# Local q and k of batches 4 to 7: loaded one token a row and transposed by DMA from SBUF instead of on TensorE

## The chip, the cores and the metric

The kernel runs on one core of one Trainium2 chip. The metric is the device time of one execution in microseconds (us); the time before is the median of three runs. Engines are called as the profile calls them: PE is TensorE (PEld its weight loads), DVE is VectorE, ACT is ScalarE, POOL is GpSimd, and SP is the engine whose queue issues most of the DMA transfers.

## What is computed

Attention with a fixed sparse mask is followed by two matrix products with a squared ReLU between them. There are 8 batches, 8 heads, 576 tokens and 64 numbers a head. Heads 0 to 3 are "local" (a token sees itself and the 31 before it), heads 4 to 7 are "strided" (it sees earlier tokens whose position is the same modulo 32).

```python
scores = scale * np.matmul(q, k.transpose(0, 1, 3, 2))
mask_local = (rel >= 0) & (rel < stride)                       # rel = query - key, stride = 32
mask_strided = (rel >= 0) & (pos[None, :] % stride == pos[:, None] % stride)
attn = softmax(np.where(masks, scores, -1e9))
x = np.matmul(attn, v).transpose(0, 2, 1, 3).reshape(4608, 512)
r = np.maximum(x @ w_in, 0.0)                                  # w_in 512 x 2048
out = (r * r) @ w_out                                          # w_out 2048 x 512
```

## The kernel before

**Units.** The attention is cut into 32 units, four a batch: unit u belongs to batch u // 4, and holds two heads. The first two of a batch are local (for batch 4, units 16 and 17), the last two strided. A unit goes through these steps, each a Python function that emits a few instructions:

- `step_T` (L188) turns q or k, which lie in SBUF with tokens on the partitions, so that the head's numbers lie on the partitions. For a local unit it is six PE transposes (L196) of 96 x 128 into PSUM, and one copy to SBUF: q by ACT (L209), k by DVE (L211) into one of the `kTl` tiles, which have 32 columns of zeros in front.
- `step_S` (L217) forms the scores: 12 (local) or 16 (strided) small matmuls (L240), exponentials on ACT (L245), masks on DVE (L251).
- `step_D` (L259), in two or three parts, multiplies with v (L276), and DVE divides by the sum (L287, L288).
- `step_E` (L291) turns the result and puts it into `xt`, the input of the matrix products: on PE for strided units (L305, copy L313), and for local units from batch 2 on by a DMA transpose from SBUF on the SP queue (L298, `xt<-x_l`).

**Loads.** `loads(b)` (L399) issues a batch's loads on SP: for each of the two local units q and k as float32 (L90, one transfer each for both heads; six consecutive tokens a partition, so that one row is 1536 bytes) and v (L137, two transfers, 256-byte rows, 96 tokens apart), then v of the strided units (L153). POOL casts them to bf16 (`cast_qk_local`, L98; L144, L145, L160). From batch 2 on the strided q and k are cast by a POOL-issued DMA into DRAM (L117), and `transpose_str` (L122) brings them back with two DMA transposes on SP (L125, `qT_s<-q_d` and `kT_s<-k_d`), the `strT` pool having two slots for each of q and k. In batches 0 and 1 strided q and k are loaded to SBUF (`load_qk_str`, L102, pool `qs_in`, two slots each) and go through `step_T`.

**Products.** The 4608 tokens are nine chunks of 512. `mm1` (L319) is one group of four 128x512 matmuls (L325), a ReLU on ACT (L328) and a square on DVE (L329); 16 such groups a chunk. `mm2` (L333) is one group of four matmuls (L340) of the second product; four of them fill one output tile of 128 rows, which ACT copies (L344) and SP stores (L346).

**Order.** The order of all engines is written by hand: what the program emits first comes first in each engine's queue, and each queue runs in that order, waiting for semaphores. There are 288 groups: chunk 0's `mm1` is groups 0 to 15, its `mm2` 16 to 31, chunk 1 has 32 to 63, chunk 2's `mm1` 64 to 79; from group 80 on `mm1` of chunk c and `mm2` of chunk c - 1 alternate, 32 groups for a chunk (80, 112, 144, 176, 208, 240). The attention steps of the batches 1 to 7 are one list (`stream_steps`, L375); `due` says how many of them stand before each group, spread evenly so that batch b's are all done where it is needed: batch 1 at group 32, batch 2 at 56, batch b from 3 on at the start of chunk b. In that list `step_T` of a local unit stands two units ahead of its scores, among the parts of `step_D`. `loads(b)` is called at group 8 for batch 2, and for b = 3 to 7 at groups 34, 58, 82, 114, 146; `transpose_str(b)` six groups later:

```python
        if n in load_at:
            loads(load_at[n])
            tr_at[n + 6] = load_at[n]
        if n in tr_at:
            transpose_str(tr_at[n])
        g()
```

SP's queue therefore holds, in program order, the loads, the y stores, the transposes of strided q and k and the `xt<-x_l` transposes.

Of the kernel before, what the change touches and what calls it, by code (L numbers as in the profile page):

```python
# [9 lines left out]
BF16 = mybir.dt.bfloat16  # L10
# [4 lines left out]
def kernel(  # L15
# [9 lines left out]
    nc = tc.nc  # L25
    B, H, S, D = q.shape
    d_model, d_ff = moe_w_in.shape
    T = B * S
# [3 lines left out]
    QL = 96  # L32
    NL = S // QL
    NJ = 8
    RH = STRIDE // NJ
    SP_ = RH * NA
# [3 lines left out]
    singles = ctx.enter_context(tc.tile_pool(name="singles", bufs=1))  # L40
    qk_st = ctx.enter_context(tc.tile_pool(name="qk_st", bufs=2))
    qk_in = ctx.enter_context(tc.tile_pool(name="qk_in", bufs=3))
    qs_in = ctx.enter_context(tc.tile_pool(name="qs_in", bufs=2))
    qkT = ctx.enter_context(tc.tile_pool(name="qkT", bufs=3))
    v_st = ctx.enter_context(tc.tile_pool(name="v_st", bufs=2))
    small = ctx.enter_context(tc.tile_pool(name="small", bufs=4))
# [4 lines left out]

    PS = bass.MemoryType.PSUM
    dram = ctx.enter_context(tc.tile_pool(name="dram", bufs=2, space=bass.MemoryType.DRAM))
    strT = ctx.enter_context(tc.tile_pool(name="strT", bufs=2))
    ps_h = ctx.enter_context(tc.tile_pool(name="ps_h", bufs=2, space=PS))
    ps_y = ctx.enter_context(tc.tile_pool(name="ps_y", bufs=1, space=PS))
# [4 lines left out]
    NV = 4  # L61
# [3 lines left out]
    vls = [singles.tile([128, 2, NL, VP], BF16, name=f"vl{i}") for i in range(NV)]  # L65
    vss = [singles.tile([SP_, NBS, VP], BF16, name=f"vs{i}") for i in range(NV)]
    vl_sts = [singles.tile([128, 2 * NL, D], FP32, name=f"vl_st{i}") for i in range(2)]
    kTl = [singles.tile([128, 32 + S], BF16, name=f"kTl{i}") for i in range(3)]
    es = [singles.tile([128, 1280], BF16, name=f"e{i}") for i in range(4)]
    xt = [singles.tile([128, T], BF16, name=f"xt{p}") for p in range(4)]  # L70
    w_in_b = singles.tile([128, 4, d_ff], BF16)
# [5 lines left out]
    units = [(b, p) for b in range(B) for p in range(H // 2)]  # L77
    st = {}

    def is_local(u):  # L80
        return units[u][1] < H // 4

    def load_qk_local(u, eng, gate=None):
        b, p = units[u]
        s = st.setdefault(u, {})
        for name, src in (("q", q), ("k", k)):
            t = qk_st.tile([QL, 2, 6 * D], FP32, name=f"{name}_st")
            if gate is not None and name == "q":
                nc.gpsimd.tensor_copy(t[0:1, 0, 0:1], gate)
            eng.dma_start(out=t, in_=src[b, 2 * p:2 * p + 2]  # L90
                          .rearrange("h (p j) d -> p h (j d)", j=6))
            s[name + "f"] = t
# [9 lines left out]
    def load_qk_str(u):  # L102
        b, p = units[u]
        s = st.setdefault(u, {})
        for name, src in (("q", q), ("k", k)):
            t = qs_in.tile([SP_, 2, NJ * D], BF16, name=f"{name}_s")
            nc.gpsimd.dma_start(out=t, in_=src[b, 2 * p:2 * p + 2]
                                .rearrange("h (p j) d -> p h (j d)", j=NJ))
            s[name] = t

    XB = 2
# [10 lines left out]
    def transpose_str(b):  # L122
        for name in "qk":
            o = strT.tile([128, NJ // 2, 4 * SP_], BF16, name=f"{name}T_s")
            nc.sync.dma_start_transpose(out=o, in_=big.pop((b, name)))  # L125
            for i in range(2):
                st.setdefault(4 * b + 2 + i, {})[name + "T"] = o[:, :, 2 * SP_ * i:2 * SP_ * (i + 1)]

    def v_slot(u):
        b, p = units[u]  # L130
        return (b * 2 + p % 2) % NV
# [52 lines left out]
    def tick():  # L184
        clock[0] += 1
        run_due(lambda x: x[0] <= clock[0])

    def step_T(u, name):  # L188
        s = st[u]
        local = is_local(u)  # L190
        n, w = (6, QL) if local else (NJ, SP_)
        src = s[name]
        src = src.rearrange("p j h d -> p (j h d)" if local else "p h c -> p (h c)")
        pt = ps_t.tile([128, S], BF16, name="pt")
        for j in range(n):
            nc.tensor.transpose(pt[:, w * j:w * (j + 1)], src[:, 128 * j:128 * (j + 1)],  # L196
                                ident[0:w, 0:w])
        if local and name == "k":
            full = kTl[u % 3]
            dst = full[:, 32:32 + S]  # L200
        else:
            full = dst = qkT.tile([128, S], BF16, name=f"{name}T")
        if local:
            o = dst.rearrange("c (p j) -> c p j", j=6)
            i = pt.rearrange("c (j p) -> c p j", j=6)
        else:
            o, i = dst, pt
        if name == "q":
            nc.scalar.copy(o, i)  # L209
        else:  # L210
            nc.vector.tensor_copy(o, i)  # L211
        s[name + "T"] = full
# [120 lines left out]
    def mm2(c, i, pool=None):  # L333
# [8 lines left out]
        if part == 3:  # L342
# [3 lines left out]
            nc.sync.dma_start(out=out[r0:r0 + 128, :], in_=y)  # L346

    T_ = lambda u, nm: (lambda: step_T(u, nm))
    S_ = lambda u: (lambda: step_S(u))
    D_ = lambda u, part: (lambda: step_D(u, part))  # L350
# [19 lines left out]
        return [(fn, 0 if i < n - 8 else 4) for i, fn in enumerate(order)]  # L370

    def has_T(u):
        return is_local(u) or units[u][0] < XB

    def stream_steps(lo, hi, base):  # L375
        order = [T_(lo, "q"), T_(lo, "k"), T_(lo + 1, "q"), S_(lo), T_(lo + 1, "k")]
        ends = {}
        for u in range(lo, hi + 1):
            if u < hi - 1:
                order.append(S_(u + 1))  # L380
            if u > lo:
                order.append(E_(u - 1))
                ends[u - 1] = base + len(order)
            if u < hi:
                order.append(D_(u, 0))
                if u + 2 < hi and has_T(u + 2):
                    order.append(T_(u + 2, "q"))
                order.append(D_(u, 1))
                if u + 2 < hi and has_T(u + 2):
                    order.append(T_(u + 2, "k"))  # L390
                if not is_local(u):
                    order.append(D_(u, 2))
        return order, ends
# [5 lines left out]
    def loads(b):  # L399
        u = 4 * b  # L400
        for i in range(2):
            load_qk_local(u + i, nc.sync, gate=gates.get(b) if i == 0 else None)
            load_v_local(u + i, nc.sync)
        load_v_str(u + 2, nc.sync)
        load_v_str(u + 3, nc.sync)
        w_out = load_w_out if b == 1 else (lambda i: None)
        if b >= XB:
            cast_str_dram(b)
        else:
            load_qk_str(u + 2)  # L410
        w_out(0)
        cast_qk_local(u, pool2)
        cast_v_local(u)
        if b < XB:
            load_qk_str(u + 3)
        w_out(1)
        cast_qk_local(u + 1, pool2)
        cast_v_local(u + 1)
        w_out(2)
        cast_v_str(u + 2)  # L420
        cast_v_str(u + 3)
        w_out(3)

    load_qk_local(0, nc.sync)
    load_qk_local(1, nc.sync)
    load_qk_str(2)
    make_identity(nc, ident)
    load_qk_str(3)
# [88 lines left out]
    load_at = {8: 2}  # L517
    tr_at = {}
# [10 lines left out]
    for n, g in enumerate(groups):  # L529
        while done < due[n]:  # L530
            steps[done]()
            done += 1
        if n in load_at:
            loads(load_at[n])
            tr_at[n + 6] = load_at[n]
        if n in tr_at:
            transpose_str(tr_at[n])
        g()
        tick()
    for _ in range(4):  # L540
# [31 lines left out]
```

## Time and profile before

| what | value |
|---|---|
| runs | 335.35, 336.91, 337.31 us; median 336.91 |
| profiled execution | 338.12 us, of which the span (first to last instruction) 336.3 |
| busy in the span | PE 305.6, DVE 175.3, ACT 167.6, POOL 88.7 us |
| L325 matmuls | 147.1 us recorded busy in 550 records |
| L340 matmuls | 100.7 us in 390 records and 41.6 us in 170 |
| L196, q of local units | 96 transposes, 7.4 us busy |
| L196, k of local units | 96 transposes, 7.5 us busy |
| L209 / L211 copies of local q / k | 0.64 us (ACT) / 0.75 us (DVE) each |
| DMA packets on the queue that SP uses | 54784, 33.63 MB |

The profiler records one execution; times within it are counted from the first instruction. In a timeline each line is a run of like instructions: start, length, engine, line of the code, operation, tile written and read, shape, count, and in brackets how long the engine had been idle and what ended that. A PE length is the time of one pass through a pipeline, so that lengths of neighbours overlap. "SPq" is SP's queue: the length there is that of the issue. A few matmul records are missing from the trace.

### The profile page before, as it was taken

To read this page: it belongs to the slowest core of one execution; us is meant where nothing else is said; L and a number is where in the kernel's file an instruction comes from. 1 tells how busy PE (TensorE), PEld (TensorE's weight loads), DVE (VectorE), ACT (ScalarE), POOL (GpSimd) and SP (SyncE) were. 2 spreads that over 40 slices of the span, in tenths; PEclk is the share of its full clock that TensorE was granted. 3 is DMA by queue.
4 is the path that set the end of the run, shared out by engine and by line. 5 is a ranking of instruction groups with operands and counts; after the bars stand their busy time and mean duration, and the time that the engine had idled before them with its cause. 6 is when DMAs were issued, how large, how long until landed. Compare 5 with 4: busy or idle time off the path is not lost.

```text
span 336.3 us, 6368 instructions
## 1 busy us (share of the span) xinstructions
PE 305.6 (91%) x2446; PEld 157.5 (47%) x2488; DVE 175.3 (52%) x424; ACT 167.6 (50%) x342; POOL 88.7 (26%) x114
## 2 busy tenths in 40 slices
PE   2689488997899999999999999999999999999995
PEld 1574235553455544455445554554445444444442
DVE  5595335546665788755676566556555422222200
ACT  4746344554764666455455545554554344443411
POOL 6154662553620744700066006400000000000000
PEclk9999879998999999999999999999999999999999
DMA  8999999999944999590199229900410001100021
GB/s 183 211 174 225 216 150 218 198 283 202 155 73 136 225 207 242 112 187 31 52 245 222 68 71 226 186 34 31 48 52 33 31 31 48 49 31 33 31 94 62
DMA packets 61085, 42.94 MB, mean 128 GB/s; under 512 B 42560, under 2 KB 53952, under 8 KB 60864
## 3 DMA queue, kind: packets, MB, share of 16 engines
q1 hardware_dynamic: 54784, 33.63, 46.8%
q0 software_dynamic: 6272, 8.92, 16.2%
q8 instruction: 19, 0.31, 0.4%
q14 instruction: 10, 0.08, 0.1%
HBM read 36.70 MB, written 12.98 MB: 148 GB/s over the span
## 4 chain that ended last, share of the span: by engine, by line
PE 69%; DMA 14%; DVE 5%; POOL 4%; SPq 3%; issue 2%; ACT 1%; POOLq 0%; ACTq 0%
PE ph L325 28%; PE py L340 25%; DMA vl_st<-in_v_dram 12%; PE ph L340 8%; PE pt L276 3%; PE pt L240 2%; DMA w_out_b<-in_moe_w_out_dram 2%; SPq L90 2%; DVE g_sb L329 2%; PE pt L196 1%; PE pt L305 1%; POOL vl L144 1%; DVE xt L313 1%; POOL vl L145 1%; SPq L137 1%
## 5 line engine op out<-in xcount | busy, mean ns | idle before, releaser
L325 PE MATMUL ph<-xt,w_in_b 128*128 128x512 bf16 x550 | 147.1, 385 | 3.2 <-DVE xt L313 1.7
L328 ACT ACTIVATE r<-ph 128x512 bf16<-128x512 f32 x144 | 86.1, 598 | 110.0 <-PE ph L325 105.4
L329 DVE TENSOR_TENSOR g_sb<-r 128x512 bf16<-128x512 bf16 x144 | 69.5, 484 | 113.0 <-ACT r L328 112.9
L340 PE MATMUL py<-w_out_b,g_sb 128*128 128x512 bf16 x390 | 100.7, 379 | 1.1 <-issue 0.8
L340 PEld LDWEIGHTS <-g_sb 128*128 128x128 bf16 x576 | 52.1, 98 | 57.1 <-issue 2.9
L325 PEld LDWEIGHTS <-w_in_b 128*128 128x128 bf16 x576 | 51.5, 99 | 50.9 <-issue 1.8
L245 ACT ACTIVATE e<-pt 72x288 bf16<-72x288 f32 (+1 forms) x128 | 47.9, 408 | 10.6 <-PE pt L240 10.6
L340 PE MATMUL ph<-w_out_b,g_sb 128*128 128x512 bf16 x170 | 41.6, 379 | 0.3
L276 PEld LDWEIGHTS <-e 72*128 72x128 bf16 (+1 forms) x448 | 25.1, 101 | 21.5 <-issue 2.8
L98 POOL CAST q_l<-q_st 96x768 bf16<-96x768 f32 x14 | 12.2, 869 | 81.9 <-DMA q_st<-in_q_dram 78.8
L288 DVE TENSOR_TENSOR x_s<-pt,rinv 72x384 bf16<-72x384 f32 (+1 forms) x48 | 24.4, 509 | 1.6
L144 POOL CAST vl<-vl_st 128x768 bf16<-128x768 f32 x16 | 14.4, 902 | 35.0 <-DMA vl_st<-in_v_dram 28.6
L251 DVE TENSOR_TENSOR e<-e,mask_str 72x576 bf16<-72x576 bf16 x32 | 18.8, 588 | 3.7 <-ACT e L245 3.6
L287 DVE RECIPROCAL rinv<-pt 96x6 f32<-96x6 f32 (+2 forms) x80 | 14.7, 184 | 11.1 <-PE pt L276 10.9
L288 DVE TENSOR_TENSOR x_l<-pt,rinv 96x384 bf16<-96x384 f32 x32 | 17.7, 553 | 1.1
L160 POOL CAST vs<-v_st 72x1024 bf16<-72x1024 f32 x15 | 17.8, 1213 | 0.4
L344 ACT COPY y<-ph 128x512 f32<-128x512 f32 x11 | 6.4, 586 | 22.5 <-PE ph L340 22.5
L209 ACT COPY qT<-pt 128x576 bf16<-128x576 bf16 x20 | 12.7, 636 | 8.2 <-PE pt L196 8.0
L344 ACT COPY y<-py 128x512 f32<-128x512 f32 x25 | 14.7, 586 | 4.1 <-PE py L340 4.1
L196 PE MATMUL pt<-ident,q_l 96*128 96x96 bf16 x96 | 7.4, 219 | 9.9 <-POOL mask_loc L446 5.2
L251 DVE TENSOR_TENSOR e<-e,mask_loc 128x576 bf16<-128x576 bf16 x32 | 14.4, 450 | 3.7 <-ACT e L245 3.7
L276 PE MATMUL pt<-vl,e 128*128 128x65 bf16 x192 | 12.3, 201 | 4.3 <-DVE e L251 2.4
(57 smaller groups left out, 176.5 us busy)
## 6 DMA issues: line engine op xcount, KB each, us to landing
out_dram<-y SPq DMA_DIRECT2D x36, 256.0 KB
q_st<-in_q_dram SPq DMA_DIRECT2D x16, 288.0 KB
k_st<-in_k_dram SPq DMA_DIRECT2D x16, 288.0 KB
vl_st<-in_v_dram SPq DMA_DIRECT2D x32, 144.0 KB
v_st<-in_v_dram SPq DMA_DIRECT2D x16, 288.0 KB
w_in_b<-in_moe_w_in_dram POOLq DMA_DIRECT2D x4, 512.0 KB, 6.7
w_out_b<-in_moe_w_out_dram POOLq DMA_DIRECT2D x4, 512.0 KB, 7.8
q_d<-in_q_dram POOLq DMA_DIRECT2D x6, 288.0 KB, 4.8
```

What stands on the lines that cost most here:

```text
L144: nc.gpsimd.tensor_copy(t[:, :, :, 0:D].rearrange("p h t d -> p (h t) d"), s["vf"])
L160: (copy or nc.gpsimd.tensor_copy)(t[:, :, 0:D], s["vf"].rearrange("p h (j d) -> p (h j) d", d=D))
L245: nc.scalar.activation(e[0:kn, lo:lo + S // 2], banks[row][half][0:kn, 0:S // 2], AF.Exp, scale=scale)
L251: nc.vector.tensor_tensor(x, x, m.to_broadcast([kn, n, w]), op=ALU.mult)
L276: nc.tensor.matmul(po[:, n - n0, :], e[0:kn, pos(n):pos(n) + 128], rhs[0:kn, src(n), 0:D + 1], start=True, stop=True)
L287: nc.vector.reciprocal(rinv[0:w, 0:m], po[0:w, 0:m, D:D + 1])
L288: nc.vector.tensor_tensor(x, po[0:w, 0:m, 0:D], rinv[0:w, 0:m].to_broadcast([w, m, D]), op=ALU.mult)
L325: nc.tensor.matmul(ph, w_in_b[:, kk, 128 * ff:128 * (ff + 1)], xt[kk][:, 512 * c:512 * (c + 1)], start=(kk == 0), stop=(kk == 3))
L328: nc.scalar.activation(r, ph, AF.Relu)
L329: later(1, lambda: nc.vector.tensor_tensor(g[:, ff, :], r, r, op=ALU.mult))
L340: nc.tensor.matmul(py, g[:, ff, 128 * j:128 * (j + 1)], w_out_b[:, ff, :], start=(ff == 0), stop=(ff == 15))
L344: nc.scalar.copy(y, py)
```

## The change

From batch `LB` = 4 on, local q and k are loaded by head with one token of 64 numbers as a row (the layout that v has: partition p holds tokens p, 96 + p, ...), cast by POOL as before, and then turned by two DMA transposes a unit on SP, q into a new pool `locT`, k straight into a `kTl` tile. The local units of batches 4 to 7 have no `step_T` any more, so that the steps left (18 instead of 22 for each of the batches 3 to 6, in whose stretch the next batch's transposes stood) are spread over the same groups. The DMA transposes of a batch's two local units are emitted 12 and 16 groups after its loads: for batch 4 at groups 70 and 74. Batches 1 to 3 keep the PE transposes (batch 0 too). There are four `kTl` tiles instead of three, and the pool `qs_in` is gone: strided q and k of batches 0 and 1 are put into slots of `strT`.

```diff
-    qs_in = ctx.enter_context(tc.tile_pool(name="qs_in", bufs=2))
+    locT = ctx.enter_context(tc.tile_pool(name="locT", bufs=4))
-    kTl = [singles.tile([128, 32 + S], BF16, name=f"kTl{i}") for i in range(3)]
+    kTl = [singles.tile([128, 32 + S], BF16, name=f"kTl{i}") for i in range(NV)]
+    LB = 4
     def load_qk_local(u, eng, gate=None):
...
+            if b >= LB:
+                for hh in range(2):
+                    eng.dma_start(out=t[:, hh].rearrange("p (t d) -> p t d", d=D),
+                                  in_=src[b, 2 * p + hh].rearrange("(t p) d -> p t d", p=QL))
+                s[name + "f"] = t
+                continue
     def load_qk_str(u):
...
-            t = qs_in.tile([SP_, 2, NJ * D], BF16, name=f"{name}_s")
+            t = strT.tile([128, NJ // 2, 4 * SP_], BF16, name=f"{name}T_s")
+            t = t.rearrange("p a c -> p (a c)")[0:SP_, 0:2 * NJ * D].rearrange("p (h c) -> p h c", h=2)
+    def transpose_local(u):
+        s = st[u]
+        for name in "qk":
+            if name == "k":
+                full = kTl[v_slot(u)]
+                dst = full[:, 32:32 + S]
+            else:
+                full = dst = locT.tile([128, S], BF16, name="qT_l")
+            nc.sync.dma_start_transpose(out=dst.rearrange("c (t p) -> c t p", p=QL),
+                                        in_=s[name].rearrange("p t h d -> p (t h d)"))
+            s[name + "T"] = full
     def step_T(u, name):
...
-            full = kTl[u % 3]
+            full = kTl[v_slot(u)]
     def has_T(u):
-        return is_local(u) or units[u][0] < XB
+        return units[u][0] < (LB if is_local(u) else XB)
...
         if n in load_at:
             loads(load_at[n])
-            tr_at[n + 6] = load_at[n]
+            if load_at[n] >= XB:
+                tr_at[n + 6] = lambda b=load_at[n]: transpose_str(b)
+            if load_at[n] >= LB:
+                for i in range(2):
+                    tr_at[n + 12 + 4 * i] = lambda u=4 * load_at[n] + i: transpose_local(u)
         if n in tr_at:
-            transpose_str(tr_at[n])
+            tr_at[n]()
```

## The prediction

> **What bounds the kernel now.** I read the page first (busy shares and slices), then the timelines of PE and of the SP queue around the edit, then the windows of a place where PE had already stood still. The page:
>
> ```profile
> PE 305.6 (91%) x2446; PEld 157.5 (47%) x2488; DVE 175.3 (52%) x424; ACT 167.6 (50%) x342; POOL 88.7 (26%) x114
> ```
>
> PE is the bound. In each 33 us stage from 131 us on, the windows give it 32.4 to 32.7 us busy, so what is taken from PE's order there comes off the end, and a PE wait there is added to it. PE's timeline, with columns start, length, form, and idle before:
>
> ```profile
> 179.54 1.03 PE L325 MATMUL ph<-xt,w_in_b 128*128 128x512 bf16 x4
> 180.41 0.42 PE L196 MATMUL pt<-ident,q_l 96*128 96x96 bf16 x6
> 180.67 1.03 PE L340 MATMUL py<-w_out_b,g_sb 128*128 128x512 bf16 x4
> ```
>
> Lengths overlap; starts tell the price. Four matmuls take 0.87 us (179.54 to 180.41), the six transposes of one operand 0.26 us (180.41 to 180.67).
>
> The SP queue where the first changed batch (4) is loaded:
>
> ```profile
> 105.03 1.38 SPq L90 DMA_DIRECT2D q_st<-in_q_dram  x1
> 106.51 0.40 SPq L90 DMA_DIRECT2D k_st<-in_k_dram  x1
> 107.00 0.95 SPq L137 DMA_DIRECT2D vl_st<-in_v_dram  x2
> ...
> 110.29 1.04 SPq L153 DMA_DIRECT2D v_st<-in_v_dram  x2
> 111.42 0.39 SPq L346 DMA_DIRECT2D out_dram<-y  x1
> 112.20 1.94 SPq L298 DMA_TRANSPOSE xt<-x_l  x1
> 114.23 0.54 SPq L346 DMA_DIRECT2D out_dram<-y  x1
> 114.87 3.95 SPq L125 DMA_TRANSPOSE qT_s<-q_d  x1
> 118.92 2.17 SPq L125 DMA_TRANSPOSE kT_s<-k_d  x1
> 121.18 1.80 SPq L298 DMA_TRANSPOSE xt<-x_l  x1
> 123.07 0.53 SPq L90 DMA_DIRECT2D q_st<-in_q_dram  x1
> ```
>
> From 105 to 123 us the queue has no hole: it works through its own list, 18 us for what PE passes in some 15. PE, at the scores of unit 16 (batch 4's first local pair):
>
> ```profile
> 120.23 1.03 PE L325 MATMUL ph<-xt,w_in_b 128*128 128x512 bf16 x4
> 121.96 0.43 PE L240 MATMUL pt<-qT,kTl 64*128 64x96 bf16 x12 [0.70 <-DVE kTl L211]
> ```
>
> And what a PE wait costs beside itself, in windows (PE busy, then the others, then PEclk) around a 4.7 us wait in batch 1:
>
> ```profile
> 38.00:41.50 3.50, 0.00 (x0) 0.00 (x0) 0.00 (x0) 0.00 (x0) 3.46 (x6) 0.76 0.95 178
> 41.50:46.00 4.50, 4.47 (x26) 1.94 (x27) 1.30 (x1) 1.54 (x3) 4.39 (x6) 0.50 1.05 141
> ```
>
> PE ran at half clock after it, until 46.65 by the clock record.
>
> **What the Trainium skill says.** "TensorE: Matmul & The Clock Gate", What's actually happening: an idle window of about 3.4 us halves PE's clock, a busy one restores it. The trace agrees (above). "Perfetto Trace Analysis", DMA Instruction — HWDGE: the recorded length of such an issue is the queue's part alone; the data moves later. The trace agrees: the xt<-x_l issue at 137.12 is 1.21 us long, and the completion updates of its semaphore end at 139.68; that at 121.18, behind a backlog, completes at 127.79. "VectorE: DVE Perf Modes", The three transpose paths: a 128x128 transpose is 390 ns on TensorE, 1309 ns by DMA. Here the six blocks of 96x128 cost PE 0.26 us, and SP 1.20 to 2.60 us an issue (12 of xt<-x_l, median 1.48). "DMA: Bandwidth & Descriptors", Why small descriptors are slow: 256-byte descriptors carry 27% overhead. The packets agree roughly: 18 ns median for 256 B, 91 for 1536 B.
>
> **Part 1, PE transposes removed.** Eight local units (16, 17, 20, 21, 24, 25, 28, 29), q and k: 16 x 0.26 = 4.2 us of PE. Eight ACT copies (0.64) and eight DVE copies (0.75) go too; ACT and DVE are at half load, so that is worth nothing but the 0.70 us wait above.
>
> **Part 2, loads.** q and k are each split by head and read in 256-byte rows as v already is: eight issues instead of four a batch. A pair of such v issues takes 0.95 us, so four more are 1.9 us of SP. In bytes, a k tile of 1536-byte rows took 1.1 us of DMA (by the completion updates q_st is there at 169.60, k_st at 170.71) and the same bytes of v 1.44 (170.71 to 172.15): 4 x 0.34 = 1.4 us, within the 1.9. The POOL casts keep their size (0.83).
>
> **Part 3, DMA transposes added.** Four a batch, of exactly xt<-x_l's form (96x768), on SP behind the stride pair's: 1.5 us of SP each, and some 2.4 us from the end of the issue to landing (1.4 quiet, 2.0 at 179.65 to 183.40, 4.8 at 121.18). So four issues and four transposes are 8 us of SP a batch. SP has that: between 149 and 166 us it mostly waits for y. The question is when they land.
>
> **Part 4, the new wait, batch 4.** I count out the order that the code makes. The loads are called at group 58, the transposes of unit 16 at group 70, and unit 16's scores fall at group 72; in between lie 14 groups x 0.87 = 12.1 and 2.0 us of attention steps. From group 58's start at 106.4, less the two removed transposes, PE is there at 120.5. In SP's order the two new transposes stand behind the loads, two y stores, the stride pair's two transposes and two xt<-x_l. That list ends at 122.98 now; four more load issues: 124.9; q and k, 2 x 1.5: 127.9; landing 2.4: 130.3 (129.2 to 132.7 with the quiet and the busy landing). PE waits 9.8 us; the scores begin at 130.3 instead of 121.96, +8.3. Behind them on PE stands everything: the rest of chunk 2's first matmul, hence ACT, DVE and y. Unit 17's transposes follow 3 us later, its scores 7 groups later: no wait. The clock: a wait of this length costs a half-clock stretch of about 5 us after it (41.53 to 46.65), so 2.5 us lost (1.7 to 3.4 for one or two windows).
>
> **Part 5, batches 5 to 7.** Here 20 groups lie between loads and scores, 20 x 0.87 + 2 = 19.3 us. Batch 5's loads run ahead of a delayed PE; its local transposes follow the stride pair, called at group 88: issue ends 147.02 now, q and k to 150, landed about 151.7, against scores 13.5 us after group 88 (140.27), at 153.8: covered by 2 us. Batch 6: the present list ends at 181.37 (started 166.14); the local transposes overtake the second xt<-x_l, so 179.56 + 1.9 + 3.0 + 1.4 = 185.9, against 167.44 + 19.3 = 186.7: covered by 0.8. Batch 7, where such an issue takes 1.2 (215.36): 215.25 + 1.9 + 2.4 + 1.4 = 221.0, against 200.66 + 19.3 = 220.0: a wait of 1.0. So I take 1 us for both, with 0 and 6 as ends. The xt<-x_l behind them lands some 3 us later and is due 11 us later: nothing.
>
> **Part 6, buffers.** Stride q and k of batches 0 and 1 take strT's two slots: transpose_str(2), issued at 60.50, must then wait for unit 6's PE transposes, over at 53.9, and transpose_str(3) (81.47) for unit 7's (60.5). Nothing; if PE were 7 us later there, SP would stall. A fourth kTl adds a 72 ns memset; nothing, DVE waits for DMA there.
>
> **Sum.** +8.3 (scores of unit 16, removals before them included) + 2.5 (clock) + 1.0 (batches 6, 7) - 14 x 0.26 (removals after them) = +8.2 us. Against the profiled span, 336.3 + 8.2 = 344.5; that execution took 338.12, 1.8 outside the span. The median of the runs is 336.91, so 345.1; the estimate's grain is a microsecond: 345.0.
>
> **Rivals.**
> - *The transposes land in time* (faster). For it: batch 6's whole present list needs 17.3 us from first issue to last landing, batch 4's 22.8. Against it: SP's list at 105 to 123 has no idle to shed. It decides at the landing of unit 16's k: by 120.5 there is no wait and the 4.2 come off, 332.7; at 125.6 (121.96 + 3.64) it is even. 10%.
> - *The wait is short, 2 to 7 us*: landing at 122.5 to 127.5, and half-clock for little of it; within 1%, around 338. Against it, SP alone is at 127.9 with issues of median length. 10%.
> - *DMA becomes the bound in every stage*: 256-byte rows and transposes share the rings with the loads (DMA share above 1 in 8 us windows after each load), the thin covers of batches 5 to 7 go, and each waits 3 to 5 us with some half clock: 345 + 10 = 355. For it: landings of 7 to 9 us behind a backlog (114.87 lands at 123.58). Against: batch 5 has no loads in front. 17%.
> - *The forecast*: one long wait at unit 16, little after: 340 to 350. 63%.
>
> That the edit does nothing isn't open: the PE lines must go.
>
> **How the numbers follow.** The forecast alone spans 340 to 350 (landing 129.2 to 132.7, clock 1.7 to 3.4, batches 6 and 7 at 0 to 3). For 8 in 10 I go to 338.5 below, into the short wait, and 353 above, into the waits of each batch. A difference under 1% (3.4 us) is about what a measurement of this kernel can't tell from no change. Faster 7%, same 12%, slower 81%: most of the first rival is faster, the short wait same, the last two slower.
>
> **What would show it.** Right: one PE idle of 8 to 12 us at the scores of unit 16, released by a DMA transpose; PEclk at 0.5 for about 5 us behind it; PE instructions fewer by 96, each stage after it 1 us shorter; SP with four more loads and four more transposes a batch. Wrong: no wait over 3 us there (then about 333), or waits of several us in three stages.

## The result, and the profile after

The changed kernel takes 351.9 us in the median of four runs (348.9 to 354.1), the kernel before 336.6 in four beside them: 1.045 times as long, with a 95% interval of 1.037 to 1.054. The profiled execution of the change took 348.93 us and spans 347.0, 10.7 more than the span before. The forecast was 345.0, slower, within 338.5 to 353.0. Here and below a median is of all runs of a kernel, while a ratio leaves out those over 1.5% above its fastest, so that the two need not agree to the last digit.

The page, busy shares first, then the PE clock in 40 slices (tenths of full speed):

```profile
span 347.0 us, 6208 instructions
...
PE 304.5 (88%) x2351; PEld 154.7 (45%) x2392; DVE 169.4 (49%) x417; ACT 163.9 (47%) x334; POOL 90.1 (26%) x114
...
PEclk9999879999999958999999989999999999999999
```

The span grew by 10.7 us while PE's busy time fell slightly: PE stands still for longer. PEld has 96 instructions fewer (2392 for 2488), the transposes that went. The clock has a new dip, from 122.8 us on by the clock record, and a small one at 198.

SP's queue where batch 4 is loaded, as shown for the kernel before:

```profile
104.22 1.78 SPq L92 DMA_DIRECT2D q_st<-in_q_dram  x2
106.09 1.00 SPq L92 DMA_DIRECT2D k_st<-in_k_dram  x2
...
111.72 0.95 SPq L174 DMA_DIRECT2D v_st<-in_v_dram  x2
112.77 0.37 SPq L367 DMA_DIRECT2D out_dram<-y  x1
113.23 1.65 SPq L319 DMA_TRANSPOSE xt<-x_l  x1
114.97 0.53 SPq L367 DMA_DIRECT2D out_dram<-y  x1
115.61 3.18 SPq L134 DMA_TRANSPOSE qT_s<-q_d  x1
118.88 2.02 SPq L134 DMA_TRANSPOSE kT_s<-k_d  x1
120.99 1.86 SPq L319 DMA_TRANSPOSE xt<-x_l  x1
122.95 1.28 SPq L146 DMA_TRANSPOSE qT_l<-q_l  x1
124.32 1.23 SPq L146 DMA_TRANSPOSE kTl<-k_l  x1
```

Again the queue has no hole, and unit 16's k is the last of the list: its issue ends at 125.55, and the completion updates of its semaphore end at 128.57. PE at that place:

```profile
118.86 1.03 PE L346 MATMUL ph<-xt,w_in_b 128*128 128x512 bf16 x4
128.61 0.66 PE L261 MATMUL pt<-qT_l,kTl 64*128 64x96 bf16 x12 [8.72 <-DMA kTl<-k_l]
129.21 1.46 PE L346 MATMUL ph<-xt,w_in_b 128*128 128x512 bf16 x3
130.89 1.91 PE L346 MATMUL ph<-xt,w_in_b 128*128 128x512 bf16 x4 [0.22 <-issue]
```

PE was there at 119.9, idled 8.72 us for `kTl<-k_l`, and started 0.04 us after it had landed. Behind the wait a line of four matmuls is 1.91 instead of 1.03 us long. The windows of the wait and of what follows (PE busy first, PEclk after POOL):

```profile
119.90:128.60 8.70, 0.00 (x0) 0.00 (x0) 2.05 (x7) 0.60 (x1) 1.88 (x3) 0.67 1.14 220
128.60:133.00 4.40, 4.17 (x26) 2.05 (x28) 0.80 (x2) 1.47 (x4) 0.38 (x1) 0.50 0.74 168
```

At half clock 4.4 us of PE's time do 2.2 us of work, so 2.2 us are lost. A second, shorter wait of the same kind stands at unit 24 (batch 6), and a very small one at unit 28:

```profile
197.56 0.43 PE L261 MATMUL pt<-qT_l,kTl 64*128 64x96 bf16 x12 [3.45 <-DMA kTl<-k_l]
197.93 1.89 PE L346 MATMUL ph<-xt,w_in_b 128*128 128x512 bf16 x4
...
231.80 0.43 PE L261 MATMUL pt<-qT_l,kTl 64*128 64x96 bf16 x12 [0.34 <-DMA kTl<-k_l]
```

Half clock follows the second one too, from 197.9 to 201.3 by the clock record: 1.7 us lost.

**The account.** The start of the kernel differs by a few us from one execution to the next: in this profile and those of experiments 1 to 6, whose programs are nearly alike up to there, the scores of unit 14 begin between 105.7 and 111.3 us. So I compare the stretch from the first score matmul of unit 14 (108.39 before, 107.59 after) to the end, which holds all sixteen removed operands (the first stood at 115.9) and every new wait: 228.0 us before, 239.4 after, +11.5 before rounding. Waits of 8.72 + 3.45 + 0.34, less the 0.70 that stood at unit 16 before, are +11.8; half clock +3.9; sixteen operands at 0.26 us, -4.2. Sum +11.5.

### The profile page after: what moved, and what is told of

Same layout as the page of the kernel before. It is cut to its first block, busy times and chain, and to the rows that moved or that the text cites. A ratio compares the mean times of both kernels' runs of the same rounds, so it can differ in the third digit from the quotient of the medians.

```text
span 347.0 us, 6208 instructions
## 1 busy us (share of the span) xinstructions
PE 304.5 (88%) x2351; PEld 154.7 (45%) x2392; DVE 169.4 (49%) x417; ACT 163.9 (47%) x334; POOL 90.1 (26%) x114
## 4 chain that ended last, share of the span: by engine, by line
PE 55%; DMA 23%; SPq 7%; POOL 5%; DVE 4%; issue 3%; ACT 2%; POOLq 0%; ACTq 0%
PE ph L346 23%; PE py L361 19%; DMA vl_st<-in_v_dram 12%; PE ph L361 7%; DMA kTl<-k_l 4%; DMA v_st<-in_v_dram 3%; SPq L98 3%; PE pt L297 2%; DMA w_out_b<-in_moe_w_out_dram 2%; SPq L158 2%; PE pt L261 2%; POOL vs L181 1%; DVE g_sb L350 1%; DMA k_st<-in_k_dram 1%; POOL vl L165 1%
## 5 line engine op out<-in xcount | busy, mean ns | idle before, releaser
L346 PE MATMUL ph<-xt,w_in_b 128*128 128x512 bf16 x559 | 149.2, 388 | 2.9 <-DVE xt L334 1.7
L361 PEld LDWEIGHTS <-g_sb 128*128 128x128 bf16 x576 | 53.1, 98 | 59.9 <-issue 4.2
L266 ACT ACTIVATE e<-pt 72x288 bf16<-72x288 f32 (+1 forms) x128 | 48.9, 407 | 24.5 <-PE pt L261 24.4
L106 POOL CAST q_l<-q_st 96x768 bf16<-96x768 f32 x14 | 13.2, 940 | 93.3 <-DMA q_st<-in_q_dram 78.1
L309 DVE TENSOR_TENSOR x_s<-pt,rinv 72x384 bf16<-72x384 f32 (+1 forms) x48 | 24.4, 509 | 1.6
L165 POOL CAST vl<-vl_st 128x768 bf16<-128x768 f32 x16 | 15.2, 953 | 25.8 <-DMA vl_st<-in_v_dram 25.2
L297 PE MATMUL pt<-vs,e 72*128 72x65 bf16 x256 | 16.2, 198 | 0.0
L261 PEld LDWEIGHTS <-kTl 64*128 64x128 bf16 x192 | 5.3, 103 | 23.2 <-DMA kTl<-k_l 14.0
```

The source lines that it names most:

```text
L165: nc.gpsimd.tensor_copy(t[:, :, :, 0:D].rearrange("p h t d -> p (h t) d"), s["vf"])
L266: nc.scalar.activation(e[0:kn, lo:lo + S // 2], banks[row][half][0:kn, 0:S // 2], AF.Exp, scale=scale)
L297: nc.tensor.matmul(po[:, n - n0, :], e[0:kn, pos(n):pos(n) + 128], rhs[0:kn, src(n), 0:D + 1], start=True, stop=True)
L309: nc.vector.tensor_tensor(x, po[0:w, 0:m, 0:D], rinv[0:w, 0:m].to_broadcast([w, m, D]), op=ALU.mult)
L346: nc.tensor.matmul(ph, w_in_b[:, kk, 128 * ff:128 * (ff + 1)], xt[kk][:, 512 * c:512 * (c + 1)], start=(kk == 0), stop=(kk == 3))
L361: nc.tensor.matmul(py, g[:, ff, 128 * j:128 * (j + 1)], w_out_b[:, ff, :], start=(ff == 0), stop=(ff == 15))
```

## The experiments

Where a kernel's span is compared below, "the tail" is that stretch from unit 14's scores to the end.

**1. From batch 5 on only**, to take the first wait away and leave the rest:

```diff
-    LB = 4
+    LB = 5
```

> The change from batch 5 on only (batch 4 keeps its old loads and PE transposes). Theory (one long wait at the scores of unit 16 because its transposes stand at the end of a full SP list, and a short one at unit 24): the wait of 8.7 us and its half clock go, the 3.4 us wait at unit 24 and its half clock stay, 12 of 16 operand transposes (3.1 us of PE) are still saved: span 338 to 339, so about 0.5% over the kernel before. Rival (the 256-byte rows and the transposes load the DMA engines in every batch): three of four changed batches are left, so at least 346.

Measured: 338.1 us, 1.004 times the kernel before (1.001 to 1.007). The tail is 227.4 (-0.5). PE at unit 24:

```profile
186.25 0.43 PE L261 MATMUL pt<-qT_l,kTl 64*128 64x96 bf16 x12 [2.53 <-DMA kTl<-k_l]
186.61 1.04 PE L346 MATMUL ph<-xt,w_in_b 128*128 128x512 bf16 x4
```

The wait at unit 16 is gone (0.43 us are left, for the k copy) and with it all but half a percent of the loss, though three of the four changed batches are left. Unit 24 still waits, but at 2.53 us the clock stays whole (four matmuls in 1.04), which the expectation had not foreseen; the last section says what set it apart. The rival falls. That the runs lie 0.4% above the kernel before, where the tail of the one profile is 0.5 us below it, stays open: the profiled execution (335.5 us) was among the three fastest of twenty.

**2. The local transposes first.** Same transfers, another place in SP's order:

```diff
-                    tr_at[n + 12 + 4 * i] = lambda u=4 * load_at[n] + i: transpose_local(u)
+                    tr_at[n + 3 + 2 * i] = lambda u=4 * load_at[n] + i: transpose_local(u)
```

> Same work as the change, but the local transposes are emitted 3 and 5 groups after the loads, ahead of the strided pair's, instead of 12 and 16. Theory (place in SP's list decides): the wait at unit 16 falls from 8.7 to 0 to 2 us, that at unit 24 to nothing, no half clock; span 332 to 335, faster than before by about 1%. Rival (DMA engines' load): the same bytes and packets move, so the time stays at 349 to 352, and the waits move to the strided units' scores.

Measured: 333.2 us, 0.988 times the kernel before (0.981 to 0.995): faster than both. SP and PE around unit 16:

```profile
113.99 1.25 SPq L146 DMA_TRANSPOSE qT_l<-q_l  x1
115.33 1.27 SPq L146 DMA_TRANSPOSE kTl<-k_l  x1
116.69 2.34 SPq L319 DMA_TRANSPOSE xt<-x_l  x1
...
123.04 1.57 SPq L134 DMA_TRANSPOSE qT_s<-q_d  x1
124.69 2.86 SPq L134 DMA_TRANSPOSE kT_s<-k_d  x1
```

```profile
119.81 1.03 PE L346 MATMUL ph<-xt,w_in_b 128*128 128x512 bf16 x4
120.99 0.34 PE L261 MATMUL pt<-qT_l,kTl 64*128 64x96 bf16 x7
121.81 0.30 PE L261 MATMUL pt<-qT_l,kTl 64*128 64x96 bf16 x5 [0.48 <-DVE x_s L309]
```

The two transposes are issued 9 us earlier, k lands at 120.94, and PE has hardly to wait. The strided pair is issued 6 to 7 us later and no scores wait for it. No transpose is waited for in batches 5 to 7. The tail is 223.9 us, -4.1, where 16 x 0.26 = 4.2 was the saving: with the waits gone the whole of it is there, although the same bytes move in the same packets. So in this order the DMA engines' load costs nothing that can be seen in the tail.

**3. POOL's casting transfers held back.** In the change's trace unit 24's k, issued at 189.54, landed only at 197.52. POOL had issued the next batch's casting transfers just ahead of it, between the issues of q and k. SP, then POOL:

```profile
188.22 1.22 SPq L146 DMA_TRANSPOSE qT_l<-q_l  x1
189.54 1.22 SPq L146 DMA_TRANSPOSE kTl<-k_l  x1
...
188.53 0.49 POOL L126 DMA_DIRECT2D q_d<-in_q_dram  x1
189.01 0.49 POOL L126 DMA_DIRECT2D k_d<-in_k_dram  x1
```

The experiment lets POOL wait for the last local transpose first:

```diff
+    dummy = singles.tile([1, 1], BF16)
...
         if b >= XB:
+            if b > LB:
+                nc.gpsimd.tensor_copy(dummy, kTl[v_slot(u - 3)][0:1, 32:33])
             cast_str_dram(b)
```

> The change, with POOL's casting transfers of the next batch (q_d, k_d) held back until the local k transposes of the batch before have landed. Theory for unit 24 (its transposes were issued at 188 to 191 and landed only at 195.7 and 197.5 because those transfers, issued at 188.5 and 189.0, shared the DMA engines): that wait goes with its half clock, and the wait at unit 16 shrinks from 8.7 to 6 or 7; span about 340. Rival (they were late by their own traffic or SP's list alone): waits as in the change, 347 or more.

Measured: 342.2 us, 1.018 times the kernel before (1.011 to 1.025); tail 234.2. SP and POOL at unit 24, then PE at units 16 and 24:

```profile
187.19 1.23 SPq L147 DMA_TRANSPOSE kTl<-k_l  x1
...
194.62 0.18 POOL L431 COPY dummy<-kTl 1x1 bf16<-1x1 bf16 x1 [7.40 <-DMA kTl<-k_l]
194.85 0.49 POOL L127 DMA_DIRECT2D q_d<-in_q_dram  x1
```

```profile
125.86 0.66 PE L262 MATMUL pt<-qT_l,kTl 64*128 64x96 bf16 x12 [7.87 <-DMA kTl<-k_l]
...
191.44 0.43 PE L262 MATMUL pt<-qT_l,kTl 64*128 64x96 bf16 x12 [0.38 <-DMA kTl<-k_l]
191.80 1.04 PE L347 MATMUL ph<-xt,w_in_b 128*128 128x512 bf16 x4
```

At unit 24 the wait falls from 3.45 to 0.38 us and the half clock is gone. From issue to landing unit 24's k takes 4.2 us here (187.19 to 191.40) instead of 8.0, its q 2.7 instead of 7.5. At unit 16 k takes 2.6 instead of 4.2, so that collision was worth some 1.7 us of landing there; the wait fell by 0.85 only, to 7.87 for the 6 or 7 expected, and what is left of it is SP's list.

**4. The rows alone.** Loads of the change, PE transposes kept:

```diff
-        return units[u][0] < (LB if is_local(u) else XB)
+        return is_local(u) or units[u][0] < XB
...
-            if load_at[n] >= LB:
-                for i in range(2):
-                    tr_at[n + 12 + 4 * i] = lambda u=4 * load_at[n] + i: transpose_local(u)
...
-        if local:
+        if local and units[u][0] < LB:
             o = dst.rearrange("c (p j) -> c p j", j=6)
```

> Only the loads of the change for batches 4 to 7 (by head, 256-byte rows), with PE transposes kept (their copies write without interleaving). Theory (the rows are hidden): 336 to 337, same as before, no wait of more than 1 us at any scores. Rival (256-byte rows slow all loads of the batch): 340 or more, POOL's casts waiting longer for q_st and k_st.

Measured: 338.0 us against 336.2 (336 to 337 was expected), 1.003 times (1.000 to 1.006), not told from no change. The tail is 227.4 (-0.5), with no wait over 0.3 us at any scores in it; that half us is the wait at unit 16 for the k copy, which writes without interleaving now (0.70 before, 0.20 here). The 256-byte rows are hidden, and so are the new buffers (four `kTl` tiles, no `qs_in`), which this run has too.

**5. Batch 4 alone:**

```diff
-            if b >= LB:
+            if b == LB:
...
-        return units[u][0] < (LB if is_local(u) else XB)
+        return units[u][0] != LB if is_local(u) else units[u][0] < XB
...
-            if load_at[n] >= LB:
+            if load_at[n] == LB:
```

> The change in batch 4 alone; batches 5 to 7 keep their loads and PE transposes. Theory: the wait at unit 16 stays at 8 to 9 us with its half clock and nothing else waits; from the scores of unit 14 to the end 237 us (228.0 before, 239.4 with the change), so 345 to 346 in all. Rival (the load on the DMA engines in all four batches): a quarter of the loss, 340 at most.

Measured: 346.0 us, 1.027 times (1.023 to 1.031); tail 235.9 (+7.9 for the 9 expected), as the wait is 7.18 us for the 8 to 9 expected.

```profile
120.03 1.03 PE L346 MATMUL ph<-xt,w_in_b 128*128 128x512 bf16 x4
128.24 0.66 PE L261 MATMUL pt<-qT_l,kTl 64*128 64x96 bf16 x12 [7.18 <-DMA kTl<-k_l]
```

One batch carries most of the loss. Experiments 1 and 5 together (-0.5 and +7.9) give 7.4, 4.1 less than the change's tail: here the wait at unit 16 is 1.5 us shorter and half clock outlives it by 3.5 us instead of 4.4 (0.4 us less lost), and in experiment 1 unit 24 waits 0.9 us less and keeps its clock (1.7). These are 1.5 + 0.4 + 0.9 + 1.7 = 4.5, near enough to 4.1.

**6. The change once more**, for a second profile:

> The changed kernel once more, for a second profile of it. The profiled execution of the change spans 347.0 us, the runs lie up to 5 us above. Theory (the waits at units 16 and 24 are set by queue order and repeat; what varies is the start, where DMA is the bound): from the scores of unit 14 to the end 239 us within 1.5 again (before: 228.0), any difference in the span lying ahead of unit 14. Rival (the waits of batches 5 to 7 vary from run to run): the stretch after unit 14 differs by 2 us or more, with other waits at units 20, 24, 28.

Measured: one execution of 350.7 us, span 348.7, tail 240.2 (239.4 in the first). The waits repeat, 7.99 us at unit 16 and 4.00 at unit 24, none at units 20 and 28, and half of the 1.7 us between the two spans (0.9) lies ahead of unit 14. The theory holds within the 1.5 us that it allowed.

**7 and 8. Local transposes first, from batch 3 and from batch 2 on:** experiment 2's edit, with `LB = 3` and `LB = 2` (the latter keeps the gate of batch 2's loads).

> Local transposes ahead of the strided pair's, and from batch 3 on instead of 4. Theory: batch 3's four operands save another 1.0 us of PE if their transposes land before unit 12's scores, 16 groups after its loads: 331 to 333. Rival (in batch 3 the loads of w and of the batches before still fill the DMA engines): a wait of several us at unit 12, 335 or more.

> The same from batch 2 on. Theory: at batch 2 the DMA engines are full (share above 1 from 24 to 80 us), its transposes land late and SP's list grows by 8 us ahead of batch 3's loads; a wait at unit 8 or later eats the 1.0 us: 333 to 337. Rival: another 1.0 us off, 330 to 332.

Measured: 333.0 us from batch 3 on, 0.989 times (0.985 to 0.993), and 334.2 from batch 2 on, 0.991 times (0.988 to 0.993). Neither is told apart from experiment 2. From batch 3 on, unit 12 starts after 0.34 us, but unit 16 waits:

```profile
117.66 0.43 PE L261 MATMUL pt<-qT_l,kTl 64*128 64x96 bf16 x12 [1.96 <-DMA kTl<-k_l]
```

From batch 2 on, units 12 and 16 wait 1.55 and 2.29 us. In experiment 7 what batch 3's transposes save is given back at batch 4: from unit 10's scores, ahead of both, to the end it is 248.7 us, as in experiment 2. In experiment 7 the wait stands at unit 16, and not at unit 12 where I had looked for it.

## Why the prediction was right, and where its size was off

**Right in kind.** The step that carried it, part 4, held: SP's list, PE's place and the wait came out as worked out. PE was at unit 16 at 119.9 (120.5 predicted), k's issue ended at 125.55 (127.9), k landed at 128.6 (130.3), PE idled 8.72 us (9.8). The queue's shares: the loads take SP 2.15 us longer (104.22 to 112.67 against 105.03 to 111.33; 1.9), the transposes 1.23 to 1.28 us each (1.5), from the end of the issue to landing 3.0 (2.4). The half clock cost 2.2 us (2.5). Experiment 2 shows that place in the queue, and not the amount of work, made the wait; experiment 3 puts some 1.7 us of k's landing down to POOL's casting transfers, which the list of part 4 did not have.

**Parts 1, 2, 6 right.** 0.26 us an operand is confirmed by the tail of experiment 2 (-4.1 for -4.2). The rows cost nothing (experiment 4). The shared strT slots cost nothing seen (experiment 4 has them): transpose_str(2) was issued at 62.81, right behind a v load that ended at 62.70.

**Part 5 mis-sized.** It allowed 1.0 us for batches 6 and 7 together; they took 3.45 + 0.34 of waiting and 1.7 of half clock, 5.5 in all. The term that failed is the "1.4" for landing in batch 6's sum: of the landings that part 3 had listed (1.4, 2.0 and 4.8) it is the quiet one. The order on SP was right: the sum had k's issue end 18.3 us after the first load, and it ended 17.5 after (190.76 - 173.29). Then it took not 1.4 but 6.8 us to land, because POOL's transfers for batch 7 came in at 188.5 (experiment 3). Both sides of this were in the trace of the kernel before, where those transfers were issued just behind SP's last transpose, which the added ones push back into them:

```profile
179.65 1.72 SPq L298 DMA_TRANSPOSE xt<-x_l  x1
...
182.92 0.49 POOL L117 DMA_DIRECT2D q_d<-in_q_dram  x1
```

I had asked what stands ahead in SP's queue, and not what another queue starts at that moment. Batch 5 did not wait, as forecast, and batch 7, which has no next batch's casts, waited 0.34 us for the 1.0.

**The sum.** In the profiled execution it is +10.7 us of span for the +8.2 forecast, and the difference is part 5's term (+4.5) less 2.0 at unit 16, whose scores began at 128.6 instead of 130.3 (0.8 of that because this execution was earlier at unit 14) and whose half clock lost 0.3 less. So a miss of 4.5 us is partly hidden by errors of the other sign. The median lies further off, 351.9 for 345.0, outside the 340 to 350 of the forecast alone: it is within the range because that had been stretched to 353 for the rival of a wait in each batch, which did not come; to that extent it is luck. The profiled execution was the fastest of the four, and the second profile shows 0.8 us more in the tail. What the other runs lose beyond that is not shown, for no profile of one exists. More half clock is little of it: their mean granted clocks are 0.966 to 0.971 against 0.970, worth 1.5 us at most.

**The rivals.** "DMA becomes the bound in every stage" comes nearest to the time (355) and is wrong: batches 5 and 7 hardly wait, and experiment 2 moves the same load faster than before. "The transposes land in time" became true, by moving them.

## What to carry to other kernels

A step that is moved from an engine to a queue arrives when the queue's list reaches it: count the list from its first entry to the landing, and count what the waiting engine does in the same time; here the list took 24.4 us to k's landing (104.22 to 128.57), PE was there after 15.7 (119.89), and 8.7 us were lost for a saving of 4.2. Then put the transfer that is needed first at the front: the same transposes nine and eleven groups earlier turned 4.5% lost into 1.2% won. And look at every queue that shares the DMA engines: a transfer that was quiet at its old time may fall, some us later, on another queue's.

## What was not expected of the hardware

Whether a short PE wait costs half clock did not go by its length alone: 3.45 and 4.00 us did, 2.53 (experiment 1) and 2.29 (experiment 8) did not, but 1.96 in experiment 7 did (half clock from 118.8 to 122.2). After the 8.72 us wait the half clock outlived it by 4.4 us.

The ten traces show what set them apart. In each of them all changes of the clock between its first and its last half clock lie a whole number of steps of 3.41 us apart, so that a grid can be laid through the execution. These are the steps of that grid in which the waits of experiments 7, 1 and 8 began (PE busy first, PEclk after POOL):

```profile
115.41:118.82 3.41, 1.45 (x18) 0.69 (x17) 2.28 (x7) 1.01 (x2) 2.99 (x4) 1.00 1.20 176
182.14:185.56 3.42, 1.58 (x8) 0.49 (x6) 0.91 (x3) 0.60 (x1) 0.00 (x0) 1.00 1.15 152
118.33:121.74 3.41, 1.77 (x12) 0.68 (x10) 3.34 (x9) 1.56 (x3) 3.29 (x4) 1.00 0.99 184
```

The wait of 1.96 us lies within one step, of which PE was busy for 1.45 us (0.42 of it), and half clock followed in the next. A border cuts the other two, so that PE was busy for 0.46 and 0.52 of the step, and none followed. Over all ten traces, from where the clock record begins (22 to 27 us) to 330 us, of 861 such steps at full clock, the 16 in which PE was busy for at most 0.43 were all followed by half clock, none with 0.48 or more was, and of three at 0.46 or 0.47 two were. So "an idle window of about 3.4 us" in the prediction asks for too much: here a wait of 2 us was enough where it fell into one step, and where the steps lie differs from one execution to the next. The trace of the kernel before had shown it too, with half clock from 80.8 to 84.2 us behind three waits of less than 1 us each in one step (PE busy for 0.46 of it). This is a count over the traces; no experiment tests it.

A transpose of 96x768 from SBUF landed 2.4 to 2.7 us after its issue began at best, and took 7.5 to 8.0 beside two casting transfers of 288 KB.
